# A new written order for a fused attention and squared-relu kernel, with the squares of its up-projection tiles moved between engines

## The chip, the cores and the metric

One core of one Trainium2 chip runs the whole program. The metric is the device time of one execution in microseconds (us), the median of several runs. Runs here differ by up to 1.4% for one kernel, so kernels are compared in runs that alternate on one chip. A ratio is the mean time of one kernel's fast runs over the mean of the other's fast runs of the same rounds, so it is not quite the ratio of the medians that stand beside it.

## The reference

```python
def _attn_ref(q, k, v):                       # q, k, v: 8 x 8 x 576 x 64
    scores = scale * np.matmul(q, k.transpose(0, 1, 3, 2))
    rel = pos[:, None] - pos[None, :]
    mask = (rel >= 0) & (rel < 64)            # a causal window of 64
    # ... softmax ...
    return np.matmul(attn, v)

def _moe_ref(x, w_in, w_out):                 # x: 4608 x 512, w_in: 512 x 2048
    h = np.maximum(x @ w_in, 0.0)
    return (h * h) @ w_out
```

Attention over a short window makes x; a two-layer network with a squared relu follows.

## The kernel before

Every piece of work is one word of a long text, and each engine executes its share of the words in the order of the text. A word's letters name the work, its numbers the tile, and what follows an @ the engine (D is DVE, A is ACT, P is POOL). Work is done in nine groups of 512 tokens. The words that matter:

- `S8`: scores of block 8 on PE; `E8.0` the exponentials on ACT; `M8.0` the mask on DVE; `V8.0` the values on PE; `N8.0` the norm on DVE.
- `U4.0` an up-projection chunk of 128 tokens (groups 0 and 1) with `R4.0`, its relu on ACT, and `Q4.0`, its square. `u2.0`, `r2.0`, `s2.0` are the same for groups 2 to 8, with 512 tokens.
- `O0.0.0`: the plain out-projection of group 0. From group 1 on it is done by seven products, `p1.1.0` and so on, whose inputs are in part sums of squares, `sa1.1.0@D`.

```python
SQUARE = "DAAP"                 # engine of the square of u tile f, by f % 4
SQUARE4 = ('DDDA', 'DADA')      # of the chunk, for group 0 and group 1

ps_up  = ctx.enter_context(tc.tile_pool(name="ps_up", bufs=2, space=bass.MemoryType.PSUM))
ps_out = ctx.enter_context(tc.tile_pool(name="ps_out", bufs=2, space=bass.MemoryType.PSUM))
ps_att = ctx.enter_context(tc.tile_pool(name="ps_att", bufs=4, space=bass.MemoryType.PSUM))

def square(key, a, b):
    # ... out: the tile of squares, hps: the up-projection in PSUM, hr: its relu in SBUF ...
    e = square_on(key, a, b)
    if e == "P":
        nc.gpsimd.tensor_tensor(out=out, in0=hr, in1=hr, op=ALU.mult)
        return
    if e == "A":
        nc.scalar.activation(out=out, in_=hr, func=AF.Square)
        return
    nc.vector.scalar_tensor_tensor(
        out=out, in0=hps[:], scalar=0.0, in1=hr, op0=ALU.max, op1=ALU.mult)
```

The square on DVE reads PSUM once more; the two others read the relu's copy. An up-projection has two PSUM buffers, so the tile after next waits until its buffer has been read for the last time.

The softmax here doesn't subtract the row's maximum and nothing guards it: scores larger than these inputs give would overflow.

Of the kernel before, what the change touches and what calls it, by code (L numbers as in the profile page):

```python
# [16 lines left out]
    lk0 lq0 dv0 ck0.0@A ck0.1@D ck0.2@P dv1 ck0.3@D W14 Tk0.0 Tk0.1 tk0.0@A li0 tk0.1@D cq0.0@A  # L17
    cq0.1@P cq0.2@D cq0.3@D Tq0.0 Tq0.1 tq0.0@A cv0@D dv2 tq0.1@D cn0@P cv1@A li1 S0 cs1@P S1
    E0.0 cn1@P E0.1 M0.0 E1.0 S2 M0.1 E1.1 M1.0 V0.0 ci0.0@P ci0.1@A dv3 V0.1 N0.0 N0.1 E2.0
    M1.1 cv2@P E2.1 li2 X0 M2.0 x0@D V1.0 cs2@P V1.1 M2.1 S3 N1.0 cn2@P U0.0@u N1.1 E3.0 E3.1 X1  # L20
    M3.0 V2.0 ci1.0@A ci1.1@P x1@D V2.1 li3 N2.0 U1.0@u R0.0 N2.1 M3.1 cv3@A X2 Q0.0 U0.1@o R1.0
    cs3@P x2@D U1.1@o Q1.0 R0.1 lo0 V3.0 Q0.1 R1.1 V3.1 U2.0@u N3.0 ci2.0@A ci2.1@P N3.1 U2.1@o
    Q1.1 R2.0 X3 Q2.0 lo1 R2.1 U0.2@u x3@D Q2.1 U1.2@u ci3.0@A ci3.1@P U3.1@o R0.2 R1.2 U0.3@o
    Q0.2 lk1 R3.1 Q1.2 U3.0@u R0.3 co0.0@D co0.1@P U2.2@u Q0.3 Q3.1 R3.0 U1.3@o R2.2 lq1 Q3.0
    Q2.2 U2.3@o R1.3 co1.0@P co1.1@D U3.2@u Q1.3 R2.3 U3.3@o R3.2 lo2 Q2.3 Q3.2 R3.3 O0.0.0
    ck1.0@D ck1.1@P ck1.2@A ck1.3@D Q3.3 O0.0.1 Tk1.0 lo3 Tk1.1 tk1.0@A O0.1.0 tk1.1@D cq1.0@P
    cq1.1@A O0.1.1 cq1.2@P cq1.3@A Tq1.0 dv4 Tq1.1 tq1.0@A tq1.1@D co2.0@P co2.1@A dv5 ta1.0@D
    S4 ta1.1@D S5 E4.0 dv6 O0.0.2 ta2.0@D E4.1 M4.0 E5.0 O0.1.2 M4.1 co3.0@P E5.1 dv7 co3.1@D S6
    M5.0 S7 M5.1 E6.0 cv4@P O0.0.3 ta2.1@D lk2 E6.1 M6.0 E7.0 cn4@P V4.0 M6.1 V4.1 E7.1 cv5@D
    O0.1.3 M7.0 Z0.0 cs5@P M7.1 N4.0 O0.2.0 Z0.1 cn5@P cv6@D lq2 N4.1 V5.0 cs6@P V5.1 ta3.0@D  # L30
    O0.3.0 cn6@P cv7@A N5.0 N5.1 V6.0 cs7@P V6.1 ta3.1@D O0.2.1 N6.0 z0.0 V7.0 N6.1 V7.1 O0.3.1
    N7.0 z0.1 N7.1 ck2.0@A ck2.1@P xx5 O0.2.2 ck2.2@D ck2.3@A ta4.0@D O0.3.2 ta4.1@D dv8 Tk2.0
    Tk2.1 tk2.0@A cq2.0@D cq2.1@P O0.2.3 cq2.2@D xx7 cq2.3@P tk2.1@D Tq2.0 Z0.2 Tq2.1 tq2.0@A
    O0.3.3 z0.2 tq2.1@D dv9 Z0.3 U4.0@u U4.1@u R4.0 z0.3 cv8@D S8 Q4.0 dv10 R4.1 cn8@P S9 E8.0
    U4.2@u E8.1 M8.0 dv11 E9.0 S10 M8.1 E9.1 M9.0 V8.0 E10.0 V8.1 M9.1 dk12 E10.1 N8.0 cv9@P
    Q4.1 M10.0 S11 M10.1 R4.2 U4.3@u N8.1 cs9@P dk13 E11.0 Q4.2 cn9@P E11.1 V9.0 V9.1 M11.0 R4.3
    cv10@P U5.0@u M11.1 dk14 N9.0 Q4.3 cs10@P N9.1 R5.0 U5.1@u cv11@D cn10@P xx9 Q5.0 cs11@P
    V10.0 R5.1 V10.1 N10.0 U5.2@u ek12@P Q5.1 N10.1 dk15 V11.0 R5.2 U5.3@u N11.0 ek13@P Q5.2
    V11.1 dq12 R5.3 p1.1.0 N11.1 Q5.3 ek14@P U6.0@u xx11 U6.1@u R6.0 p1.1.1 Q6.0 R6.1 dq13
    U6.2@u Q6.1 ek15@P va1.0 dq14 U6.3@u R6.2 p1.2.0 Q6.2 eq12@P R6.3 dq15 U7.0@u Q6.3 U7.1@u  # L40
    Kk3 R7.0 p1.2.1 Q7.0 R7.1 eq13@P sa1.3.0@D U7.2@u Q7.1 vc1.0 dv12 U7.3@u eq14@P R7.2
    sa1.3.1@D Q7.2 R7.3 vz1.0 eq15@P u2.0 sa1.1.0@D Q7.3 dv13 sa1.1.1@D u2.1 r2.0 sa1.2.0@D Kq3
    sa1.2.1@D r2.1 sa1.4.0@D s2.1 p1.6.0 sa1.4.1@D cv12@P p1.6.1 s2.0 dv14 cn12@P p1.7.0 va1.1
    dv15 u2.2 cv13@P u2.3 r2.2 cs13@P dk16 cn13@P p1.7.1 s2.2 r2.3 S12 dk17 va1.2 s2.3 S13 E12.0
    u2.8 E12.1 cv14@P M12.0 dk18 E13.0 u2.9 M12.1 E13.1 cs14@P M13.0 r2.8 V12.0 cv15@P M13.1
    dk19 V12.1 r2.9 S14 N12.0 cn14@P p1.5.0 N12.1 E14.0 s2.8 cs15@P E14.1 dq16 V13.0 ek16@P
    M14.0 V13.1 s2.9 u2.10 M14.1 N13.0 ek17@P dq17 N13.1 u2.11 r2.10 V14.0 s2.10 ek18@P V14.1
    N14.0 xx13 S15 r2.11 N14.1 u2.4 E15.0 s2.11 E15.1 p1.5.1 M15.0 r2.4 dq18 ek19@P M15.1 u2.5
    s2.4 eq16@P va1.3 dq19 V15.0 r2.5 u2.6 N15.0 s2.5 vc1.3 eq17@P V15.1 p1.4.0 r2.6 Kk4 N15.1
    s2.6 u2.7 u2.12 r2.7 vz1.3 p1.4.1 eq18@P r2.12 xx15 s2.7 p1.3.0 s2.12 vc1.2 eq19@P u2.13  # L50
    dv16 u2.14 r2.13 vz1.2 p1.3.1 s2.13 r2.14 Kq4 u2.15 sa2.1.0@D s2.14 sa2.3.0@D p2.1.0 r2.15
    sa2.2.0@D u3.0 s2.15 dv17 sa2.3.1@D sa2.4.0@D p2.1.1 r3.0 cv16@P sa2.1.1@D dv18 u3.1 va2.0
    s3.0 cn16@P sa2.2.1@D u3.2 r3.1 dv19 vc1.1 s3.1 sa2.4.1@D p2.2.0 r3.2 vz1.1 s3.2 S16 dk20
    S17 E16.0 cv17@P u3.3 E16.1 M16.0 cs17@P E17.0 dk21 p2.2.1 M16.1 E17.1 cv18@P M17.0 r3.3
    V16.0 M17.1 cn17@P V16.1 dk22 u3.8 N16.0 cs18@P N16.1 p2.6.0 vc2.0 cv19@P r3.8 dk23 cn18@P
    V17.0 s3.8 V17.1 cs19@P S18 N17.0 p2.6.1 ek20@P N17.1 vz2.0 E18.0 s3.3 E18.1 p2.7.0 M18.0
    xx17 va2.1 ek21@P S19 M18.1 u3.9 E19.0 dq20 ek22@P E19.1 u3.10 M19.0 r3.9 M19.1 V18.0 dq21
    s3.9 V18.1 ek23@P N18.0 p2.7.1 r3.10 N18.1 s3.10 u3.11 dq22 va2.2 u3.4 r3.11 dq23 p2.5.0
    s3.11 r3.4 p2.5.1 s3.4 eq20@P Kk5 u3.5 sa3.1.0@D eq21@P va2.3 u3.6 r3.5 sa3.2.0@D dv20 V19.0
    s3.5 vc2.3 V19.1 eq22@P p2.4.0 r3.6 N19.0 s3.6 N19.1 vz2.3 u3.7 eq23@P xx19 u3.12 r3.7  # L60
    p2.4.1 s3.7 r3.12 Kq5 p2.3.0 s3.12 vc2.2 u3.13 cv20@P u3.14 vz2.2 r3.13 cn20@P dv21 p2.3.1
    s3.13 r3.14 u3.15 sa3.3.0@D s3.14 dv22 sa3.3.1@D p3.1.0 r3.15 sa3.4.0@D u4.0 s3.15 dv23
    vc2.1 S20 r4.0 sa3.1.1@D u4.1 vz2.1 E20.0 s4.0 E20.1 p3.1.1 dk24 M20.0 r4.1 cv21@P M20.1 S21
    sa3.2.1@D s4.1 V20.0 cs21@P dk25 E21.0 V20.1 sa3.4.1@D u4.2 cv22@P E21.1 M21.0 va3.0 N20.0
    cn21@P p3.2.0 dk26 M21.1 r4.2 cs22@P N20.1 u4.3 s4.2 cv23@P dk27 p3.2.1 cn22@P r4.3 cs23@P
    u4.8 vc3.0 ek24@P dq24 p3.6.0 s4.3 r4.8 V21.0 s4.8 vz3.0 ek25@P V21.1 S22 N21.0 dq25 u4.9
    N21.1 E22.0 ek26@P E22.1 p3.6.1 M22.0 r4.9 xx21 M22.1 u4.10 ek27@P s4.9 va3.1 p3.7.0 r4.10
    dq26 eq24@P u4.11 s4.10 V22.0 dq27 r4.11 V22.1 N22.0 S23 N22.1 s4.11 p3.7.1 E23.0 Kk6 E23.1
    u4.4 M23.0 eq25@P va3.2 u4.5 M23.1 r4.4 p3.5.0 s4.4 dv24 r4.5 eq26@P u4.6 s4.5 dv25 p3.5.1
    eq27@P r4.6 V23.0 s4.6 sa4.1.0@D Kq6 V23.1 u4.7 N23.0 N23.1 p3.4.0 r4.7 sa4.2.0@D u4.12  # L70
    va3.3 s4.7 xx23 vc3.3 p3.4.1 cv24@P r4.12 u4.13 s4.12 vz3.3 cn24@P vc3.2 cv25@P dv26 p3.3.0
    r4.13 cs25@P u4.14 s4.13 cn25@P vz3.2 p3.3.1 r4.14 dv27 u4.15 s4.14 sa4.3.0@D sa4.3.1@D dk36
    u5.0 r4.15 sa4.4.0@D S24 s4.15 r5.0 vc3.1 p4.1.0 dk37 E24.0 s5.0 cv26@P E24.1 u5.1 M24.0
    M24.1 cs26@P vz3.1 p4.1.1 sa4.1.1@D r5.1 cn26@P dk38 sa4.2.1@D V24.0 s5.1 cv27@P V24.1 S25
    va4.0 N24.0 u5.2 sa4.4.1@D cs27@P dk39 E25.0 N24.1 ek36@P E25.1 p4.2.0 M25.0 r5.2 M25.1 dl28
    u5.3 s5.2 ek37@P p4.2.1 r5.3 dl29 u5.8 s5.3 vc4.0 dl30 p4.6.0 ek38@P r5.8 V25.0 s5.8 V25.1
    ek39@P S26 vz4.0 N25.0 u5.9 N25.1 E26.0 dl31 E26.1 eq28@P p4.6.1 M26.0 r5.9 M26.1 xx25 u5.10
    s5.9 va4.1 eq29@P p4.7.0 r5.10 Kk9 u5.11 s5.10 eq30@P V26.0 r5.11 V26.1 N26.0 S27 N26.1
    s5.11 p4.7.1 E27.0 dv36 E27.1 u5.4 M27.0 eq31@P va4.2 dv37 u5.5 M27.1 r5.4 p4.5.0 s5.4 r5.5
    Kq7 u5.6 s5.5 p4.5.1 r5.6 dv38 V27.0 s5.6 sa5.1.0@D V27.1 cv36@P u5.7 N27.0 N27.1 p4.4.0  # L80
    dv39 r5.7 sa5.2.0@D cv37@P u5.12 va4.3 s5.7 xx27 vc4.3 p4.4.1 r5.12 u5.13 s5.12 vz4.3 vc4.2
    p4.3.0 r5.13 dk40 cv38@P u5.14 s5.13 vz4.2 p4.3.1 r5.14 cv39@P dk41 u5.15 s5.14 sa5.3.0@D
    sa5.3.1@D S28 r5.15 dk42 u6.0 sa5.4.0@D E28.0 s5.15 vc4.1 E28.1 p5.1.0 r6.0 M28.0 vz4.1
    M28.1 u6.1 ek40@P sa5.1.1@D dk43 s6.0 p5.1.1 r6.1 sa5.2.1@D V28.0 s6.1 dv40 V28.1 sa5.4.1@D
    ek41@P S29 va5.0 u6.2 N28.0 E29.0 N28.1 dv41 E29.1 p5.2.0 M29.0 ek42@P r6.2 M29.1 u6.3 s6.2
    dv42 p5.2.1 r6.3 ek43@P dv43 u6.8 vc5.0 s6.3 p5.6.0 r6.8 cv40@P vz5.0 V29.0 s6.8 V29.1 Kk10
    u6.9 N29.0 cv41@P N29.1 p5.6.1 r6.9 cv42@P u6.10 s6.9 xx29 va5.1 p5.7.0 r6.10 cv43@P u6.11
    s6.10 dk32 p5.7.1 r6.11 dk33 u6.4 s6.11 va5.2 S30 r6.4 dk34 S31 E30.0 u6.5 s6.4 E30.1 M30.0
    E31.0 dk35 p5.5.0 M30.1 E31.1 M31.0 V30.0 r6.5 M31.1 V30.1 ek32@P dq32 u6.6 N30.0 s6.5 N30.1
# [25 lines left out]
def kernel(  # L115
# [10 lines left out]
    B, H, S, D = q.shape  # L126
    NT, DM = out.shape
    DFF = moe_w_in.shape[1]
    P = 128
# [27 lines left out]
    SQUARE = "DAAP"  # L157
    SQUARE4 = ('DDDA', 'DADA')
# [552 lines left out]
```

## Time and profile before

| | before |
|---|---|
| time, median of 3 runs | 308.19 us |
| PE, ACT, DVE, POOL busy | 94%, 60%, 69%, 45% of the span |
| PE's own work, at the spacing of its starts | 282.4 us |
| where PE's gaps lie | before 116 us |

PE executes 3198 matmuls and is the engine to watch. Its busy time contains each matmul's latency, so a small gap hides in it. I therefore use a second measure: the time lost in a stretch is its length less PE's work in it, priced as the prediction tells (its list of prices leaves out 112 transposes, the 6.2 us that its sum of 282.4 us has more). Over the program before, the profiled run lost 13.8 us up to U4.0 (of which some 7 us are the wait for the first load), 6.6 us from U4.0 to p2.1, 0.9 us from p2.1 to p8.1.

### The profile page before, as it was taken

The numbers are of one execution on the slowest core, as the hardware profiler recorded it, in microseconds if no ns is written. First come the engines' busy times: TensorE is split into PE (matmuls) and PEld (weight loads), VectorE is DVE, ScalarE is ACT, GpSimd is POOL, SyncE is SP. The second block draws the span as 40 slices with busy tenths as digits, with TensorE's granted clock in tenths as the row PEclk, the third lists the DMA queues.
The fourth block names the chain that finished last, engine by engine and source line by source line (L and its number), as shares of the span: only waits on it lengthen the run. The fifth ranks groups of instructions, "written<-read, shape, count | busy, mean of one in ns | idle before, by whom it ended". The sixth has DMA issues, their size and how long they took to land.

```text
span 308.1 us, 7884 instructions
## 1 busy us (share of the span) xinstructions
PE 289.9 (94%) x3198; PEld 200.3 (65%) x3198; DVE 211.7 (69%) x437; ACT 185.7 (60%) x319; POOL 139.2 (45%) x186
## 2 busy tenths in 40 slices
PE   8589987989979999999999999999999999999994
PEld 3469954578956465666666666666666656666683
DVE  3698679877296948974966696668496396633563
ACT  2667886386657656666766576566565665665500
POOL 3454354353246725943773595445353561111110
PEclk9659999998999999999999999999999999999999
DMA  7999999997989799999999999999999911310323
GB/s 240 305 359 367 355 273 289 177 233 143 173 205 206 136 179 236 212 183 239 248 191 204 227 207 201 211 234 217 219 181 232 219 38 36 104 34 2 68 70 102
DMA packets 159524, 59.76 MB, mean 194 GB/s; under 512 B 140544, under 2 KB 154880, under 8 KB 159488
## 3 DMA queue, kind: packets, MB, share of 16 engines
q1 hardware_dynamic: 159488, 59.26, 86.0%
q8 instruction: 25, 0.41, 0.6%
q14 instruction: 11, 0.09, 0.1%
HBM read 38.80 MB, written 9.44 MB: 157 GB/s over the span
## 4 chain that ended last, share of the span: by engine, by line
PE 75%; DVE 12%; DMA 5%; ACT 3%; POOL 1%; issue 1%; SPq 0%; DVEq 0%; ACTq 0%
PE pps L580 31%; PE hps L417 29%; PE hps L408 7%; DVE pm L354 4%; PE av L365 3%; DVE h_sum L540 3%; DMA kq_st<-in_q_dram 3%; DMA st<-in_v_dram 2%; PE sc L339 2%; DVE x_sb L376 2%; DVE h L450 1%; ACT pm L348 1%; PE ops L464 1%; ACT hrelu L429 1%; PE run_ps L297 1%
## 5 line engine op out<-in xcount | busy, mean ns | idle before, releaser
L429 ACT ACTIVATE hrelu<-hps 128x512 f32<-128x512 f32 x144 | 86.0, 598 | 78.8 <-PE hps L417 64.5
L417 PE MATMUL hps<-xT,w_in 128*128 128x512 f16 x448 | 111.9, 379 | 1.5 <-DVE h L450 1.5
L445 POOL TENSOR_TENSOR h<-hrelu 128x512 f16<-128x512 f32 x28 | 31.7, 1131 | 80.9 <-ACT hrelu L429 80.9
L417 PEld LDWEIGHTS <-w_in 128*128 128x128 f16 x448 | 42.1, 98 | 35.7 <-issue 1.9
L580 PEld LDWEIGHTS <-h_sum 128*128 128x128 f16 x512 | 49.3, 98 | 16.4 <-DVE h_sum L540 1.7
L580 PE MATMUL pps<-w_sum,h_sum 128*128 128x256 f16 x384 | 48.6, 273 | 0.9 <-DVE h_sum L540 0.9
L450 DVE SCALAR_TENSOR_TENSOR h<-hps,hrelu 128x512 f16<-128x512 f32 x48 | 32.8, 687 | 23.8 <-ACT hrelu L429 23.6
L580 PEld LDWEIGHTS <-h 128*128 128x128 f16 x384 | 37.0, 98 | 11.9 <-DVE osp L598 0.3
L448 ACT ACTIVATE h<-hrelu 128x512 f16<-128x512 f32 x68 | 43.0, 633 | 2.0
L348 ACT ACTIVATE pm<-sc 128x512 f16<-128x512 f32 x72 | 38.2, 605 | 8.0 <-PE sc L339 7.9
L540 DVE TENSOR_TENSOR h_sum<-h 128x1024 f16<-128x1024 f16 x32 | 23.9, 764 | 27.0 <-PE pps L580 26.1
L408 PE MATMUL hps<-xT,w_in 128*128 128x128 f16 x512 | 34.0, 230 | 0.3 <-ACT hrelu L429 0.3
L408 PEld LDWEIGHTS <-w_in 128*128 128x128 f16 x512 | 31.9, 103 | 1.1 <-issue 0.3
L580 PE MATMUL pps<-w_out,h 128*128 128x256 f16 x256 | 32.5, 273 | 0.0
L376 DVE TENSOR_TENSOR x_sb<-av,rden 128x256 f16<-128x256 f32 x72 | 30.6, 425 | 2.5
L354 DVE TENSOR_TENSOR pm<-pm,mask_inner 128x512 f16<-128x512 f16 x56 | 31.9, 599 | 0.1
L282 POOL CAST v_ev<-st 128x512 f16<-128x512 f32 x32 | 23.0, 723 | 15.8 <-DMA st<-in_v_dram 13.9
L598 DVE SCALAR_TENSOR_TENSOR osp<-pps,ws 128x512 f32<-128x512 f32 x32 | 21.9, 683 | 7.4 <-PE pps L580 7.4
L591 DVE SCALAR_TENSOR_TENSOR ws<-pps,ws 128x512 f32<-128x512 f32 x24 | 16.4, 684 | 12.6 <-PE pps L580 12.6
L286 POOL COPY v_od<-v_ev 64x512 f16<-64x512 f16 x24 | 18.0, 751 | 11.8 <-DVE v_ev L282 7.0
L365 PEld LDWEIGHTS <-pm 128*64 128x64 f16 x576 | 14.0, 115 | 13.3 <-issue 6.9
L271 POOL CAST k<-st 128x512 f16<-128x512 f32 x28 | 18.8, 690 | 7.1 <-DMA st<-in_k_dram 6.7
(63 smaller groups left out, 282.9 us busy)
## 6 DMA issues: line engine op xcount, KB each, us to landing
st<-in_v_dram SPq DMA_DIRECT2D x40, 256.0 KB, 4.3
st<-in_k_dram SPq DMA_DIRECT2D x28, 256.0 KB, 4.7
out_dram<-osp SPq DMA_DIRECT2D x28, 256.0 KB, 3.5
st<-in_q_dram SPq DMA_DIRECT2D x20, 256.0 KB, 4.6
w_st<-in_moe_w_in_dram SPq DMA_DIRECT2D x4, 1024.0 KB, 10.1
w_st<-in_moe_w_out_dram SPq DMA_DIRECT2D x4, 1024.0 KB, 9.0
kq_st<-in_k_dram SPq DMA_DIRECT2D x3, 1024.0 KB, 6.5
kq_st<-in_q_dram SPq DMA_DIRECT2D x3, 1024.0 KB, 7.6
```

Of the source, the lines that this page charges most:

```text
L348: nc.scalar.activation(out=pm[:], in_=live["s", i][hh][:], func=AF.Exp, scale=1.0 / float(D) ** 0.5)
L354: nc.vector.tensor_tensor(out=pms[i, hh][:], in0=pms[i, hh][:], in1=mask[:], op=ALU.min)
L365: nc.tensor.matmul(av[64 * blk:64 * blk + 64, h % 4, 0:65], pms[i, h % 2][:, h // 2, blk, :], vv[:, h, 0:65], start=True, stop=True)
L376: nc.vector.tensor_tensor(out=xs[i // 2][:, 2 * half:2 * half + 2, i % 2, :].rearrange("p c (b d) -> p c b d", d=D), in0=av[:, :, 0:D].rea ...
L408: nc.tensor.matmul(hps[:, f, :], w_in_q[fq][:, c, f * P:(f + 1) * P], xT_of(i // 4)[:, i % 4 // 2, c, a:a + P], start=(c == 0), stop=(c == ...
L417: nc.tensor.matmul(hps[:], w_in_q[f // 4][:, c, f % 4 * P:(f % 4 + 1) * P], xT_of(g)[:, :, c, :], start=(c == 0), stop=(c == DMC - 1))
L429: nc.scalar.activation(out=hrelu[:] if key == "U" else hrelu[:].rearrange("p (f t) -> p f t", t=P), in_=hps[:], func=AF.Relu, scale=H_SCAL ...
L445: nc.gpsimd.tensor_tensor(out=out, in0=hr, in1=hr, op=ALU.mult)
L448: nc.scalar.activation(out=out, in_=hr, func=AF.Square)
L450: nc.vector.scalar_tensor_tensor(out=out, in0=hps[:], scalar=0.0, in1=hr, op0=ALU.max, op1=ALU.mult)
L540: eng.tensor_tensor(out=out, in0=in0, in1=in1, op=op)
L580: nc.tensor.matmul(live["p", g, k][:, m, :], lhs, rhs, start=(f == 0), stop=(f == 7))
```

## The change

The intent was to lay the order out anew, with DVE taken as slower than the model had it, and to have fewer squares on DVE. Nearly every line of the text changed; matmuls and tiles stayed. Of the 1408 words 39 also changed their engine, all of them casts or copies. Cut to its core:

```diff
-SQUARE = "DAAP"
-SQUARE4 = ('DDDA', 'DADA')
+SQUARE = "AAAA"
+SQUARE4 = ('ADDA', 'AADA')
 ...
-    R5.3 p1.1.0 N11.1 Q5.3 ek14@P U6.0@u xx11 U6.1@u R6.0 p1.1.1 Q6.0 R6.1 dq13 U6.2@u Q6.1 ...
-    p1.2.1 Q7.0 R7.1 eq13@P sa1.3.0@D U7.2@u Q7.1 vc1.0 dv12 U7.3@u eq14@P R7.2 sa1.3.1@D ...
-    u2.0 sa1.1.0@D Q7.3 dv13 sa1.1.1@D u2.1 r2.0 sa1.2.0@D Kq3 sa1.2.1@D r2.1 sa1.4.0@D s2.1 p1.6.0
+    U6.1@u Q7.3 N11.0 eq12@P p1.1.0 R6.1 xx11 U6.0@u Q6.1 U6.2@u R6.0 dq15 p1.1.1 ...
+    p1.2.0 R7.2 U7.1@u Q7.2 dv12 u2.0 sa1.1.0@D R7.1 dv13 p1.2.1 Q7.1 sa1.2.0@D eq15@P r2.0
+    sa1.1.1@D u2.1 s2.0 Kq3 sa1.3.1@D u2.2 r2.1 sa1.2.1@D s2.1 sa1.4.0@D p1.6.0 ...
```

The PE words from the two texts (cut at p1.1.0):

```
old: U4.0 U4.1 S8 S9 U4.2 S10 V8.0 V8.1 S11 U4.3 V9.0 V9.1 U5.0 U5.1 V10.0 V10.1 U5.2 V11.0 U5.3 V11.1
new: U4.0 U4.3 U4.1 U4.2 S9 U5.2 S8 U5.1 V9.0 S10 U6.3 V8.0 V9.1 V8.1 U5.3 V10.0 V10.1 U5.0 S11 U7.0 U7.3 V11.1 V11.0 U6.1
```

## The prediction

> **What bounds the kernel now.** I read the totals and the 40 slices first, then PE's waits, then the busy times per stage, then the groups that the change touches.
>
> ```profile
> PE 289.9 (94%) x3198; PEld 200.3 (65%) x3198; DVE 211.7 (69%) x437; ACT 185.7 (60%) x319; POOL 139.2 (45%) x186
> PE   8589987989979999999999999999999999999994
> ACT  2667886386657656666766576566565665665500
> PEclk9659999998999999999999999999999999999999
> ```
>
> PE is the bound, and its gaps lie in the first twelve slices (some 90 us) and in the last one. Who PE waits for, after 90 us and before:
>
> ```profile
> PE av L365 <- DVE x_sb L376: 1.3, 4, 0.5
> PE pps L580 <- DVE h_sum L540: 0.9, 1, 0.9
> PE hps L417 <- DVE h L450: 0.7, 1, 0.7
> PE sc L339 <- DVE x_sb L376: 0.2, 1, 0.2
> ...
> PE run_ps L297 <- ACT q L265: 1.9, 1, 1.9
> PE av L365 <- POOL v_od L286: 1.5, 3, 0.6
> PE warm L457 <- DVE gate L652: 1.3, 1, 1.3
> ```
>
> After 90 us PE waits 3.1 us in 218, always for DVE. I cut the span at PE's first instruction of each stage: first four-chunk up-projection (U0.0), first plain out-projection (O0), second group's up-projection (U4.0), first product (p1.1), second group of products (p2.1), last group (p8.1). The windows view (stretch, length, then busy us of PE, weight loads, DVE, ACT, POOL, granted clock, DMA):
>
> ```profile
> 0.00:19.20 19.20, 13.41 (x146) 7.78 (x146) 11.39 (x36) 9.24 (x14) 9.12 (x20) 0.77 0.99 285
> 19.20:37.30 18.10, 18.10 (x304) 17.67 (x301) 13.76 (x32) 14.15 (x24) 6.21 (x7) 0.87 1.05 364
> 37.30:61.60 24.30, 21.28 (x260) 12.29 (x258) 21.12 (x45) 15.35 (x25) 11.70 (x14) 1.00 1.00 253
> 61.60:76.00 14.40, 12.97 (x257) 11.57 (x255) 11.51 (x29) 10.53 (x20) 6.93 (x11) 0.88 0.86 189
> 76.00:116.10 40.10, 37.72 (x439) 26.45 (x434) 26.77 (x52) 26.21 (x46) 19.45 (x26) 1.00 0.99 180
> 116.10:291.50 175.40, 173.87 (x1697) 113.71 (x1696) 118.49 (x236) 109.03 (x190) 84.59 (x108) 1.00 0.84 173
> 291.50:308.10 16.60, 12.59 (x113) 10.78 (x111) 8.62 (x14) 1.19 (x2) 1.20 (x1) 0.98 0.27 80
> ```
>
> From 116 us to 291 us PE has no gap worth a change: nothing gained on another engine can show there. All there is to win lies in the first 116 us.
>
> **What can be won.** Busy time flatters PE, since a matmul's latency counts, so I price PE's work by the spacing of starts in the timeline: 0.864 us for a four-matmul up tile or out-projection step, 0.875 us for half a product, 0.9 us for a 16-matmul chunk, 0.41 us for scores of a block, 0.25 us for half its values, 6 us for the warm-up. Over the program that is 282.4 us, before and after alike: the change has the same 3198 matmuls. The other 308.1 - 282.4 = 25.7 us are the tail after the last matmul (4.0), and 21.7 us of start, waits and half clock. Of these some 7 us pass until k has come and is cast, and no order saves them. So the most that a new order could give is about 14 us; a realistic one gives a third of it.
>
> **What the Trainium skill says.**
> - "ScalarE: Activation LUTs", What ACT_TABLE_LOAD costs: an ACTIVATE with immediate scale and bias takes 186 ns + 0.833 ns per element, 613 ns at 512. The trace has 633 ns (square) and 598 ns (relu): it agrees. Relu, square and exp share one table set here, for the trace has a single table load: no reload is added.
> - "GPSIMD Engine Reference", Engine selection: elementwise work with two inputs is about twice as slow on GPSIMD as on VectorE. Here 1131 ns against 687 ns, 1.65 times.
> - "SBUF — State Buffer", Who interferes with whom: a DVE instruction with two SBUF inputs contends with a GpSimd one that reads SBUF. The trace agrees: masks take 414 ns where no POOL instruction overlaps and 652 ns where one does; the 1024-wide sums 687 and 840 ns.
>
> **The change, part by part.** The code puts all 112 squares of the plain up tiles (groups 2 to 8) on ACT; the short description speaks of POOL too, but no square is left there. The groups concerned:
>
> ```profile
> L429 ACT ACTIVATE hrelu<-hps 128x512 f32<-128x512 f32 x144 | 86.0, 598 | 78.8 <-PE hps L417 64.5
> L445 POOL TENSOR_TENSOR h<-hrelu 128x512 f16<-128x512 f32 x28 | 31.7, 1131 | 80.9 <-ACT hrelu L429 80.9
> L450 DVE SCALAR_TENSOR_TENSOR h<-hps,hrelu 128x512 f16<-128x512 f32 x48 | 32.8, 687 | 23.8 <-ACT hrelu L429 23.6
> L448 ACT ACTIVATE h<-hrelu 128x512 f16<-128x512 f32 x68 | 43.0, 633 | 2.0
> L354 DVE TENSOR_TENSOR pm<-pm,mask_inner 128x512 f16<-128x512 f16 x56 | 31.9, 599 | 0.1
> ```
>
> Of the 112, 28 leave DVE and 28 leave POOL. Of the 32 four-chunk squares 20 were on DVE and are 12. So POOL loses 28 x 1.131 = 31.7 us and falls to about 107; DVE loses 36 x 0.687 = 24.7 us and falls to about 187, or less, as its masks and sums meet fewer POOL reads (if 40 of them go from 0.65-0.84 to 0.41-0.69 us, some 8 us more). ACT gains 64 x 0.633 = 40.5 us and goes to about 226 us, 73% of the span, most loaded after PE. A square on ACT also frees its PSUM buffer at the end of the relu, 0.69 us earlier than one on DVE, which reads PSUM again.
>
> The order decides where this falls. I walked through both written orders and summed each engine's work between the same landmarks (PE / ACT / DVE in us, durations from the trace; before, then after):
> - start to U0.0: 10.7 / 8.6 / 11.1, then 10.9 / 11.0 / 10.9. A chain of load, cast, transpose, scores, exp, values, norm. One more v tile (256 KB) is loaded ahead of the first weights, and three blocks of scores come before U0.0. Before 19.2 us; I take 20.0.
> - U0.0 to O0: 16.1 / 16.4 / 15.0, then 16.7 / 18.8 / 13.0. Before 18.1 us. ACT is now the longest: 19.0.
> - O0 to U4.0: 21.1 / 16.7 / 25.1, then 19.7 / 15.7 / 21.2. Before 24.3 us, set by DVE. Now DVE and PE nearly level: 21.5.
> - U4.0 to p1.1: 10.8 / 11.5 / 12.5, then 14.9 / 18.1 / 12.2. Before 14.4 us. Four more chunks come ahead of p1.1, and ACT sets the pace: 18.0.
> - p1.1 to p2.1: 36.9 / 27.4 / 27.4, then 32.5 / 28.2 / 21.1. Before 40.1 us, 3.2 lost, largely to DVE. Less DVE and less POOL: 34.0, so 1.5 lost.
> - p2.1 to p8.1: PE 174.6, then 175.5; ACT 115.7, then 146.0 (83% of PE's). Before 175.4 us, 0.8 lost. DVE's load falls, ACT's queue is fuller: 176.5.
> - p8.1 to the end: the same chain of products and sums, 16.6.
>
> Sum: 20.0 + 19.0 + 21.5 + 18.0 + 34.0 + 176.5 + 16.6 = **305.6 us**, 2.6 us (0.8%) below 308.19. (The profiled span, 308.1, and the median agree, so I take the sum as a time.) Most of ACT's 40 us and all of POOL's 32 us therefore lie beside PE and cost or give nothing; the gain is the DVE work taken from two early stages, partly paid back where ACT takes over.
>
> **The rivals.**
> 1. *ACT becomes the bound.* ACT works in order, and a relu behind a square and two exps holds a PSUM buffer of which there are two. From U4.0 to p2.1 ACT has 46.3 us of work for PE's 47.4. For it: 97% there, and 89% from p3.1 to p4.1 (26.4 for 29.7). Against: before, PE lost 0.3 us at most to ACT relus, with ACT two thirds as loaded as PE in the middle; and I compared, for each up tile, PE's work between a buffer's two uses with ACT's and DVE's work in its way: from p2.1 on 2 of the tiles fall short, by 1.2 us in all (before: none). If it comes, each group loses 1 us more: 310 to 313 us.
> 2. *The order is simply better.* It was laid out with DVE reckoned slower than modelled, which is what the contention above asks for. The head's waits (21.7 us less 7) could fall by half: 300 to 302 us. Against: the three sets of such covers that I summed (up buffers, product buffers, scores to values) fall short by 19.4 us before and 16.3 after, which is only 3 us better, and chains of the first 20 us stay.
> 3. *Nothing shows.* PE has no gap in 175 us of 308, and the head is set by loads and by the half clock (0.5 granted from 10.4 to 24.1 us): 307 to 309 us.
>
> **Range and chances.** Rivals 1 and 3 pull up, 2 down, each stage estimate is good to about 1 us and the head to 2: 301.5 to 311 us, 8 in 10. Faster by 2% means under 302.0, which needs rival 2 nearly whole: 0.14. Slower means over 314.4, which needs rival 1 in every group: 0.05. Within 2%: 0.81.
>
> **What would show it right or wrong.** Right: ACT 224 to 228 us busy, 132 squares at about 633 ns, no POOL square, DVE below 187 with masks under 560 ns in the mean; U4.0 about 60.5 us, p2.1 about 112.5, and the last two stages unchanged. Wrong: PE waits for ACT relus or exps of more than 3 us after 116 us (rival 1); p2.1 before 109 us (rival 2); masks still near 600 ns, which would say that the casts and not the squares were what DVE met; or a second stretch of half clock in the head, 1.7 us each.

## The result

The changed kernel took 304.69 us in the median of 4 runs (303.55 to 305.72), the kernel before 308.29 us in 4 (307.87 to 308.62). The ratio is 0.9883, with a 95% interval of 0.9845 to 0.9921: 1.2% faster, within the 2%.

The page of the changed kernel: totals, then the busy tenths of 40 slices.

```profile
PE 287.6 (95%) x3198; PEld 196.4 (65%) x3198; DVE 187.1 (62%) x395; ACT 220.7 (73%) x386; POOL 107.8 (36%) x161
...
PE   7489997999999999999999999999999999999994
...
ACT  2879975699799679578886785688865887877710
...
PEclk9759999999999999999999999999999999999999
```

PE has gaps in the first seven slices alone (some 50 us) and in the last. ACT is at 5 to 9 tenths through the middle, POOL and DVE are freer. Whom PE waits for, after 60 us and then before it:

```profile
PE pps L580 <- DVE osp L598: 0.4, 1, 0.4
PE av L365 <- DVE rden L375: 0.3, 1, 0.3
PE av L365 <- DVE x_sb L376: 0.2, 1, 0.2
...
PE run_ps L297 <- ACT q L265: 2.1, 1, 2.1
PE ops L464 <- POOL w_out L278: 1.7, 1, 1.7
```

No wait for an ACT relu is left in the list. The same seven stages as in the prediction, in the windows view (stretch, length, busy us of PE, weight loads, DVE, ACT, POOL, granted clock, DMA share, GB/s):

```profile
0.00:19.30 19.30, 12.30 (x150) 7.58 (x151) 11.45 (x38) 11.62 (x19) 8.21 (x19) 0.79 0.98 283
19.30:37.30 18.00, 17.75 (x314) 17.47 (x313) 11.57 (x25) 15.98 (x28) 6.57 (x8) 0.94 1.04 365
37.30:59.30 22.00, 20.06 (x236) 10.50 (x234) 17.70 (x39) 14.55 (x24) 12.47 (x15) 1.00 1.02 275
59.30:74.90 15.60, 15.29 (x331) 13.95 (x329) 11.56 (x28) 15.04 (x28) 9.76 (x15) 1.00 1.25 199
74.90:107.80 32.90, 32.54 (x368) 22.56 (x366) 20.86 (x42) 26.87 (x49) 13.27 (x21) 1.00 1.08 206
107.80:285.40 177.60, 177.24 (x1702) 113.45 (x1701) 106.22 (x214) 134.27 (x238) 57.48 (x84) 1.00 0.85 172
285.40:301.80 16.40, 12.43 (x113) 10.86 (x111) 7.74 (x12) 2.34 (x4) 0.00 (x0) 0.99 0.27 81
```

From U4.0 to p2.1 (the fourth and fifth rows) the changed kernel takes 48.5 us, the kernel before took 54.5. PE's work there is nearly the same, 47.4 and 47.7 us. ACT is busy 15.0 of 15.6 us in the fourth row, and yet PE hardly waits. The groups that the change touches:

```profile
L429 ACT ACTIVATE hrelu<-hps 128x512 f32<-128x512 f32 x144 | 85.3, 595 | 47.5 <-PE hps L417 43.4
...
L448 ACT ACTIVATE h<-hrelu 128x512 f16<-128x512 f32 x132 | 82.7, 634 | 3.3
...
L354 DVE TENSOR_TENSOR pm<-pm,mask_inner 128x512 f16<-128x512 f16 x56 | 29.4, 550 | 7.0 <-ACT pm L348 6.7
```

The 132 squares on ACT take 634 ns each, as foretold. The POOL squares are gone.

This table holds the argument of the rest: the time lost in the one profiled run, by stretch (length less PE's priced work), with the ratio to the kernel before from all the timed runs. Of the 6.6 us of the kernel before, up to 1.7 are a second stretch of half clock (3.4 us long), of which more below.

| kernel | lost to U4.0 | U4.0 to p2.1 | p2.1 to p8.1 | median us | ratio to before (95%) |
|---|---|---|---|---|---|
| before | 13.8 | 6.6 | 0.9 | 308.3 | 1 |
| changed | 11.9 | 1.1 | 2.2 | 304.7 | 0.988 (0.985 to 0.992) |
| changed, control | 12.9 | 0.9 | 2.6 | 305.2 | 0.988 (0.985 to 0.991) |
| new order, old squares | 13.5 | 3.5 | 5.6 | 310.7 | 1.007 (1.003 to 1.010) |
| old order, new squares | 13.2 | 5.8 | 0.6 | 308.1 | 0.997 (0.995 to 1.000) |
| new to p2.1, then old | 13.1 | 1.3 | 1.2 | 303.7 | 0.985 (0.983 to 0.988) |
| old to p2.1, then new | 12.9 | 4.4 | 2.8 | 309.1 | 1.003 (1.001 to 1.006) |
| old to U4.0, then new | 13.0 | 1.4 | 2.7 | 305.6 | 0.992 (0.989 to 0.995) |
| new to U4.0, then old | 12.5 | 5.4 | 1.1 | 309.6 | 1.004 (1.000 to 1.009) |
| new from U4.0 to p2.1 alone | 14.5 | 1.7 | 1.1 | 304.5 | 0.987 (0.984 to 0.989) |

The five rows that mix the two orders all have the new squares.

### The profile page after: what moved, and what is told of

It reads as the page before. It is cut to its first block, busy times and chain, and to the rows that moved or that the text cites. A ratio compares the mean times of both kernels' runs of the same rounds, so it can differ in the third digit from the quotient of the medians.

```text
span 301.8 us, 7861 instructions
## 1 busy us (share of the span) xinstructions
PE 287.6 (95%) x3198; PEld 196.4 (65%) x3198; DVE 187.1 (62%) x395; ACT 220.7 (73%) x386; POOL 107.8 (36%) x161
## 4 chain that ended last, share of the span: by engine, by line
PE 80%; DVE 6%; DMA 6%; ACT 3%; SPq 2%; issue 1%; POOL 1%; ACTq 0%
PE pps L580 32%; PE hps L417 31%; PE hps L408 6%; PE av L365 5%; DMA w_st<-in_moe_w_out_dram 3%; PE ops L464 3%; PE sc L339 2%; DMA st<-in_v_dram 2%; DVE pm L354 2%; ACT hrelu L429 2%; SPq L183 1%; DVE h_sum L540 1%; DVE h L450 1%; ACT h L448 1%; POOL w_out L278 1%
## 5 line engine op out<-in xcount | busy, mean ns | idle before, releaser
L417 PE MATMUL hps<-xT,w_in 128*128 128x512 f16 x448 | 110.5, 380 | 0.0
L448 ACT ACTIVATE h<-hrelu 128x512 f16<-128x512 f32 x132 | 82.7, 634 | 3.3
L417 PEld LDWEIGHTS <-w_in 128*128 128x128 f16 x448 | 41.8, 98 | 35.7
L282 POOL CAST v_ev<-st 128x512 f16<-128x512 f32 x36 | 25.5, 708 | 69.2 <-DMA st<-in_v_dram 56.8
L354 DVE TENSOR_TENSOR pm<-pm,mask_inner 128x512 f16<-128x512 f16 x56 | 29.4, 550 | 7.0 <-ACT pm L348 6.7
L408 PE MATMUL hps<-xT,w_in 128*128 128x128 f16 x512 | 32.5, 223 | 0.3 <-DVE xT L393 0.2
L580 PE MATMUL pps<-w_out,h 128*128 128x256 f16 x256 | 31.7, 273 | 0.4 <-DVE osp L598 0.4
L376 DVE TENSOR_TENSOR x_sb<-av,rden 128x256 f16<-128x256 f32 x72 | 30.5, 424 | 2.5
L408 PEld LDWEIGHTS <-w_in 128*128 128x128 f16 x512 | 30.4, 100 | 0.9 <-issue 0.2
L365 PEld LDWEIGHTS <-pm 128*64 128x64 f16 x576 | 14.0, 112 | 16.7 <-issue 8.5
L271 POOL CAST k<-st 128x512 f16<-128x512 f32 x28 | 18.1, 659 | 15.7 <-DMA st<-in_k_dram 14.9
L271 POOL CAST q<-st 128x512 f16<-128x512 f32 x24 | 14.8, 616 | 21.3 <-DMA st<-in_q_dram 21.1
L375 DVE RECIPROCAL rden<-av 128x4 f32<-128x4 f32 x72 | 12.6, 175 | 13.6 <-PE av L365 13.5
L365 PE MATMUL av<-v_ev,pm 128*64 128x65 f16 x384 | 20.1, 202 | 0.5 <-DVE pm L354 0.4
```

The source lines that it names most:

```text
L271: copier(e)(out=kq16(key, i // 4)[:, :, i % 4, :].rearrange("p a (b d) -> p a b d", d=D), in_=st[key, i][:].rearrange("p (a b) d -> p a b ...
L282: copier(e)(out=v_evs[slot(i)][:, :, 0:D], in_=st["v", i][:])
L354: nc.vector.tensor_tensor(out=pms[i, hh][:], in0=pms[i, hh][:], in1=mask[:], op=ALU.min)
L365: nc.tensor.matmul(av[64 * blk:64 * blk + 64, h % 4, 0:65], pms[i, h % 2][:, h // 2, blk, :], vv[:, h, 0:65], start=True, stop=True)
L376: nc.vector.tensor_tensor(out=xs[i // 2][:, 2 * half:2 * half + 2, i % 2, :].rearrange("p c (b d) -> p c b d", d=D), in0=av[:, :, 0:D].rea ...
L408: nc.tensor.matmul(hps[:, f, :], w_in_q[fq][:, c, f * P:(f + 1) * P], xT_of(i // 4)[:, i % 4 // 2, c, a:a + P], start=(c == 0), stop=(c == ...
```

## The experiments

Theory A said that the squares taken from DVE make the gain; theory B, that the new order does; theory C, that fewer POOL reads do, since DVE and POOL get in each other's way. First the changed kernel again, as a control on the same chip.

> The changed kernel once more, as the control that the next three are compared with on one chip. Every theory: a ratio to the kernel before of 0.985 to 0.992, ACT 220 us busy, DVE 187 us, POOL 108 us. What may differ is where the half clock falls in the first 25 us; if the stretch of half clock near 68 us of the kernel before comes and goes between runs, it is chance and not the change.

It ran 305.18 us against 309.12 us, a ratio of 0.9878, so the result repeats. The eleven runs of the kernel before in the rounds of the control had granted clocks of 0.970 to 0.994. The two lowest, 0.970 and 0.971, took 310.2 and 310.1 us, the others 307.3 to 309.4. Of its 22 runs beside the later experiments two more were so low (0.972 and 0.971; 309.3 and 310.1 us). The profiled run of before, with its second stretch of half clock from 68.4 to 71.8 us, is one of the low kind (0.971, 309.83 us). The second stretch seems to come by chance in a few runs; a mean clock doesn't tell where the half clock lay, so this is inferred. It is part of the profile of before, but not of its median, and so not what the change removed.

**The order without the squares, and the squares without the order.**

```diff
 # in the changed kernel
-SQUARE = "AAAA"
-SQUARE4 = ('ADDA', 'AADA')
+SQUARE = "DAAP"
+SQUARE4 = ('DDDA', 'DADA')
```

> The new written order with the squares on the engines of before (20 of the four-chunk ones and 28 of the plain ones on DVE, 28 on POOL). Theory A, the squares taken from DVE make the gain: about 308 us, ratio 0.997 to 1.005, DVE back at some 211 us busy. Theory B, the order itself makes it: 304 to 305.5 us, ratio 0.985 to 0.991. Theory C, fewer POOL reads make it: like A, with the masks and sums of DVE slower than in the changed kernel. My guess is 306.5, a half each.

```diff
 # in the kernel before
-SQUARE = "DAAP"
-SQUARE4 = ('DDDA', 'DADA')
+SQUARE = "AAAA"
+SQUARE4 = ('ADDA', 'AADA')
```

> The old written order with the squares of the changed kernel (all plain ones on ACT, 12 of the four-chunk ones on DVE). Theory A: 304.5 to 306 us, ratio 0.986 to 0.993, the gain without the new order. Theory B: 308 us or more, since ACT then has 46 us of squares and relus more at places that were laid out for less of it; PE waits for ACT relus would appear after 116 us. My guess is 307.

The new order with the old squares is slower than the kernel before: 310.74 us, ratio 1.0067. The old order with the new squares gains next to nothing: 308.11 us, 0.9974. My guesses of 306.5 and 307 were both too low. (The squares took ACT 40 us more in the second, 83.1 for 43.0, not the 46 of my expectation.) Neither A nor B is right alone: each half is worth nothing or less, and the two together 1.2%.

PE's waits after 60 us in the new order with the old squares:

```profile
PE hps L417 <- DVE h L450: 1.4, 3, 0.6
PE pps L580 <- DVE osp L598: 1.2, 1, 1.2
PE hps L408 <- DVE h L450: 0.9, 1, 0.9
PE av L365 <- DVE pm L354: 0.5, 1, 0.5
```

PE waits for squares on DVE, which hold the up-projection's PSUM buffer longer than the new order allows. For comparison, the stretch from 60 us to p2.1, first before, then in the old order with new squares:

```profile
PE pps L580 <- DVE h_sum L540: 0.9, 1, 0.9
PE sc L339 <- DVE x_sb L376: 0.9, 2, 0.8
PE hps L417 <- DVE h L450: 0.8, 1, 0.8
PE av L365 <- DVE x_sb L376: 0.5, 2, 0.3
```

```profile
PE pps L580 <- DVE h_sum L540: 1.1, 2, 0.7
PE av L365 <- DVE x_sb L376: 0.8, 3, 0.3
PE sc L339 <- DVE x_sb L376: 0.7, 1, 0.7
PE hps L417 <- DVE h L450: 0.5, 1, 0.5
```

DVE has less work in this stretch (33.2 us busy instead of 38.3), yet PE waits for the same four things for about as long. These waits are for chains: relu, square and sum before a product; exp, mask, values and norm before the next scores take the buffers. In the old order with the new squares DVE stood idle for 2.5 us before the masks that start at 64.4 us and for 2.6 us before the sums that start at 83.2 us. It then ran through with hardly a gap to 67.2 and 89.4 us, where PE's waits for x_sb and h_sum end. So the squares that were taken away had not been in the way of these two, and a lighter DVE doesn't shorten them. Other work for PE in between can cover them.

**POOL's share.**

```diff
 # in the changed kernel
-SQUARE = "AAAA"
+SQUARE = "AAAP"
```

> The changed kernel with one plain square in four back on POOL (28 of them), DVE as changed. Theory C, POOL reads slow DVE: at least half of the gain lost, 306 us or more, masks and 1024-wide sums longer by 5 per cent or more. Theories A and B: within 0.3 per cent of the changed kernel, since PE does not wait for POOL and ACT has room again; if ACT were near its bound in the changed kernel, it would even be faster by 1 us.

It ran 306.16 us, 0.9916 to the kernel before, against the control's 0.9878 in the same rounds: some 1.2 us slower, a third of the gain, with intervals that just overlap. The group of masks, first with POOL's squares back, then in the old order with the new squares:

```profile
L354 DVE TENSOR_TENSOR pm<-pm,mask_inner 128x512 f16<-128x512 f16 x56 | 37.7, 703 | 4.7 <-ACT pm L348 4.5
```

```profile
L354 DVE TENSOR_TENSOR pm<-pm,mask_inner 128x512 f16<-128x512 f16 x56 | 27.6, 513 | 3.8 <-ACT pm L348 3.6
```

28 squares on POOL lengthen the masks from 550 ns (567 in the control) to 703 ns, and DVE is busy 195.3 us instead of 187.1. So theory C's mechanism is there, but it costs only some 0.4%: a part of the whole and not the gain.

**Where in the order the gain lies.** Each of these kernels takes one text up to a word and then what is left of the other text, in its order. All have the new squares. Theory D: the new order pays between U4.0 and p2.1, and costs a little after it. Theory E: it pays because it was laid out as one.

```diff
 # the changed kernel's text up to p2.1.0, then the old text's remaining words
 ... u2.14 s2.13 vz1.2 p1.3.1 Kq4 r2.14
-p2.1.0 s2.14 sa2.1.0@D u2.12 sa2.3.0@D dv16 sa2.2.0@D ...
+u2.12 r2.12 s2.12 dv16 sa2.1.0@D s2.14 sa2.3.0@D p2.1.0 ...
```

> Squares as changed; the new order up to the second group of products (p2.1), and from there what is left in the old order. Theory D, the order pays between U4.0 and p2.1 only (PE lost 5.8 us there with the old order and new squares, 0.9 us in the control) and costs some 2 us after p2.1 (0.6 us lost with the old order, 2.6 with the new): 303 us, ratio 0.981, faster than the changed kernel by some 2 us. Theory E, the new order pays everywhere because it was laid out as one: 305 us or more, the cut itself costing.

```diff
 # the old text up to p2.1.0, then the new text's remaining words
 ... r2.14 Kq4 u2.15 sa2.1.0@D s2.14 sa2.3.0@D
-p2.1.0 r2.15 sa2.2.0@D u3.0 s2.15 ...
+r2.15 s2.15 p2.1.0 sa2.2.0@D p2.1.1 sa2.3.1@D u3.0 ...
```

> The reverse: the old order up to p2.1, the new one after it, squares as changed. Theory D: slower than both parents, about 310 us, ratio 1.003, 5 us lost between U4.0 and p2.1 and 2 to 2.6 us after p2.1. Theory E: between the parents, 306 to 307 us.

```diff
 # the old text up to U4.0, then the new text's remaining words
 ... O0.3.3 z0.2 tq2.1@D dv9 Z0.3
-U4.0@u U4.1@u R4.0 z0.3 cv8@D S8 ...
+U4.0@u z0.3 U4.3@u R4.0 Q4.0 cv8@P R4.3 U4.1@u ...
```

> The old order up to the second group's up-projection (U4.0, some 61 us), the new one after it, squares as changed. Theory D: as the changed kernel, 305 to 306 us, ratio 0.988 to 0.991, since the new order of the first 60 us gains next to nothing (13.2 us lost before U4.0 with the old order, 12.9 with the new). If the order of the first 60 us is what pays: 308 us.

```diff
 # the new text up to U4.0, then the old text's remaining words
 ... Tq2.0 Z0.3 Tq2.1 tq2.0@D
-U4.0@u tq2.1@A z0.3 U4.3@u xx7 R4.0 Tk2.1 ...
+Tk2.1 xx7 tk2.1@D tq2.1@D U4.0@u U4.1@u R4.0 z0.3 ...
```

> The new order up to U4.0 and the old one after it, squares as changed. Theory D: as the old order with new squares, 307.5 to 308.5 us, ratio 0.995 to 0.999, and 5 to 6 us lost between U4.0 and p2.1. If the order of the first 60 us is what pays: 305 us.

Measured: 303.69, 309.13, 305.57 and 309.61 us. Theory D foretold 303, about 310, 305 to 306, and 307.5 to 308.5; the last is 1 us too low. Four of that kernel's six runs had low clocks (0.971 to 0.978) and took 309.5 to 311.7 us; the two at 0.981 and 0.982 took 307.9 and 307.4, as foretold. As the table shows, the time lost between U4.0 and p2.1 is 0.9 to 1.7 us wherever the new order stands there, and 4.4 to 5.8 us wherever the old one does with the same squares. What lies before U4.0 makes no such difference. After p2.1 the new order loses 2.2 to 2.8 us and the old one 0.6 to 1.2.

The first of the four was meant to beat both kernels. Its runs lie between 303.0 and 303.9 us, the lowest median, though its ratio (0.9854) overlaps with the changed kernel's (0.9878 and 0.9883), and they weren't timed in the same rounds. I call it the best measured, not shown to be better.

**That stretch alone, and the squares piece by piece.**

```diff
 # the old text; from U4.0 to p2.1.0 the new text's words; then the old text's remaining words
 ... O0.3.3 z0.2 tq2.1@D dv9 Z0.3
+U4.0@u z0.3 U4.3@u R4.0 Q4.0 cv8@P ...   # new text
 ...
+u2.12 r2.12 s2.12 dv16 sa2.1.0@D s2.14 sa2.3.0@D p2.1.0 ...   # old text again
```

> Squares as changed; the old order everywhere but from U4.0 to p2.1, where the new one stands: one part of the reordering alone. Theory D (that stretch is what pays): 303.5 to 304.5 us, ratio 0.985, with at most 1.5 us lost in the stretch where the old order loses 5.8. If the rest of the new order is needed too: 306 us or more.

It ran 304.45 us, ratio 0.9868: the new order of this one stretch, with the new squares, brings the whole gain. (The stretch also has `cv8` and `cv11` on POOL instead of DVE, two casts of about 0.4 us; that part wasn't tried alone.) PE's waits there are down to this (line numbers of this kernel are three lower: its L405, L362, L372 and L373 are L408, L365, L375 and L376 of the changed kernel):

```profile
PE hps L405 <- DVE h L447: 0.3, 1, 0.3
PE av L362 <- DVE x_sb L373: 0.3, 1, 0.3
PE av L362 <- DVE rden L372: 0.3, 1, 0.3
```

The wait for h_sum and the wait of the scores for x_sb are gone. DVE is busy 31.7 us in it, close to the 33.2 of the old order with the same squares.

```diff
 # in the changed kernel
-SQUARE = "AAAA"
+SQUARE = "DAAA"
```

> The changed kernel with one plain square in four back on DVE (28 of them), POOL and the four-chunk squares as changed. The new order with all old squares is 1.9 per cent (5.6 us) slower than the changed kernel, and POOL's 28 alone cost 0.4 per cent (1.0 us). If DVE's load in the later groups is what the new order can't bear, this one takes most of the other 4.6 us: 308 us or more, with PE waiting for DVE squares after 110 us. If the four-chunk squares do: within 1 us of the changed kernel.

```diff
 # in the changed kernel
-SQUARE4 = ('ADDA', 'AADA')
+SQUARE4 = ('DDDA', 'DADA')
```

> The changed kernel with the four-chunk squares (groups 0 and 1) on the engines of before, so 8 more of them on DVE in the first 110 us and none else. If the head's DVE load is what counts: 307 us or more, all of it lost before p2.1. If the later groups': within 1 us of the changed kernel. My guess is 306.5, with 1.5 us lost before p2.1, as ACT gets 5 us less there and was close to its bound.

With 28 plain squares back on DVE the time is 305.76 us (0.9924); with 8 chunk squares back it is 308.00 us (0.9986). I had guessed 306.5 for the second, and had named both outcomes for the first. On the face of it eight squares of the first two groups, 5.5 us of DVE work, cost more than 28 of the later ones, 19.2 us of it. Measured from the control's 0.988 the three parts cost 0.4% (POOL), 0.4% (plain on DVE) and 1.1% (chunks), which adds up to the 1.9% by which the new order with all the old squares is slower than the control. (These two ran in another call than the control, so each is good to about 0.4%.) The wait that the chunks bring, after 58 us:

```profile
PE hps L408 <- DVE h L450: 1.2, 1, 1.2
```

In its profiled run 1.1 us of the delay was already there at U0.0 (20.6 us against the control's 19.5), ahead of any square, and the first half clock lasted 13.7 us instead of 10.2. Its stretches therefore overstate the chunks' part. The timed runs may do so too: all six had clocks of 0.975 to 0.978, against 0.981 to 0.989 for five of the control's six. Set against the two runs of the kernel before with low clocks in the same rounds (0.971 and 0.977; 310.09 and 309.49 us), the ratio would be about 0.995 and not 0.9986. A low mean clock doesn't always cost time, though: the runs of "new to p2.1, then old" at 0.974 to 0.977 were no slower than those at 0.982 and 0.983. So the chunk squares cost something, PE's wait of 1.2 us for one of them shows it, but how much of the 1.1% is theirs stays open, and with it whether they cost more than the later ones.

**A trial that failed.**

```diff
 # the old text up to O0.0.0; then the new text's remaining words up to p2.1.0; then the old ones
 ... U3.3@o R3.2 lo2 Q2.3 Q3.2 R3.3
-O0.0.0 ck1.0@D ck1.1@P ck1.2@A ck1.3@D Q3.3 O0.0.1 ...
+ck1.0@P ck1.1@A ck1.2@D ck1.3@P Tk1.0 Tk1.1 tk1.0@D tk1.1@A O0.0.0 ...
```

> Squares as changed; old order up to O0 (there 35.7 us in two runs, against 37.3 to 38.3 with the new), new order from O0 to p2.1, old order after it. If stages add up as theory D has it: 302 us, ratio 0.979, better than any so far by 1.5 us. If the first 36 us are set by loads, so that what comes early waits later: 303.5 to 304.5 us, as the new order up to p2.1 with the old one after it.

It took 307.48 us, 3 us more than the worse of my two cases. The stages did not add up. PE's waits from 36 to 62 us (line numbers again three lower than in the changed kernel):

```profile
PE av L362 <- DVE pm L351: 3.2, 3, 2.0
PE run_ps L294 <- ACT k L262: 1.1, 1, 1.1
```

Part of the loss is the cut's own: it puts the transposes of the second group's k ahead of O0.0.0, where PE waits 1.1 us for the cast of k. O0.0.0 starts at 38.5 us, against 35.7 to 35.9 in the three other profiles with the old order up to there and a first half clock of the same 10.2 us. Later PE stood still for 2.0 us for masks that DVE was doing at about 0.77 us each instead of 0.41, and the clock was then halved from 53.6 to 57.0 us. The control's masks are as slow there (four in 3.07 us), and it has a wait of 1.4 us for them; the changed kernel's first profile has one of 1.7 us for a weight cast on POOL, in nearly the same place. One might think that the loads set the pace there and that each order only chooses which wait shows it. But the DMA share is 1.03 up to 36 us and only 0.86 from 36 to 62 us in the failed trial, against 0.99 to 1.04 in the control and the changed kernel, which speaks against it for this run. The wait for k, the waits for masks and the half clock after them are what its trace shows. The half clock alone can't be the reason: of the six timed runs five had clocks of 0.969 to 0.978, but the sixth, at 0.983, took the longest, 308.35 us. Why the masks came so late for PE stays open.

## Why the prediction was right or wrong

The time was foretold as 305.6 us and came out at 304.69, in the range and on the right side. The cause that it gave was wrong, and errors that went opposite ways helped the number. By its steps:

| stage | predicted us | changed | control |
|---|---|---|---|
| start to U0.0 | 20.0 | 19.3 | 19.5 |
| U0.0 to O0 | 19.0 | 18.0 | 18.4 |
| O0 to U4.0 | 21.5 | 22.0 | 22.3 |
| U4.0 to p1.1 | 18.0 | 15.6 | 15.8 |
| p1.1 to p2.1 | 34.0 | 32.9 | 32.5 |
| p2.1 to p8.1 | 176.5 | 177.6 | 178.1 |
| p8.1 to the end | 16.6 | 16.4 | 16.4 |
| sum: the span | 305.6 | 301.8 | 303.0 |

- **PE as the bound, and no gain after 116 us: right.** The stretch from p2.1 on even became 2 us longer, 0.9 us of it work that the new order has there, the rest lost.
- **"Four more chunks come ahead of p1.1, and ACT sets the pace: 18.0": the mis-sized term.** It took 15.6 us. ACT's words of this stage do have 18.4 us of durations in the trace (18.1 foretold), and only one of them, the square `Q7.3`, was still to start when p1.1 began. But successive activations overlap in the records: 17.6 us of durations within the stage make 15.0 us of busy time. So ACT did run nearly full, and the sum of durations, without the overlap, overstated it by some 2.6 us.
- **The base.** I took the span of 308.1 us for the median of 308.19. A run's time is about 1.7 us above its span (303.55 for 301.8, 309.83 for 308.1), so the profile of before was of a run slower than the median, with its second stretch of half clock. This and the last point went opposite ways: the stages summed to 3.8 us too many against the first profile's span, while the time was 0.9 us off. That it came so close is in part luck.
- **"The gain is the DVE work taken from two early stages": wrong as a cause.** I put the 3.2 us lost from p1.1 to p2.1 "largely to DVE", because DVE is what the waits name. With DVE's work taken away and the old order kept, 5.8 us were still lost from U4.0 to p2.1. With the new order in that stretch alone, 1.7 us were. What the waits named was the last link of a chain, and the order of that stretch is what saved the time. That it did so by putting PE work beside the chain fits the texts (3.5 us of it instead of 1.7 between the last chunk of group 1 and p1.6.0, the first product that needs the sums of squares) and the waits that went away, but no run moved that work alone. The squares were needed as well, since the new order has no room for a DVE square that holds a PSUM buffer (3.5 us lost there with the old squares).
- **Engine sums: right but for ACT.** POOL 107.8 us (foretold about 107), DVE 187.1 (about 187 or less), ACT 220.7 (224 to 228). ACT's groups grew by the 40 us that I reckoned: the squares went from 43.0 to 82.7. Its busy time grew by 35.0, since successive activations overlap in the records: the durations of all ACT instructions sum to 198.9 us before and 241.3 after, and 116 and 192 pairs of them overlap, by 13.1 and 20.6 us in all. That is 7.5 us over 76 more pairs, 98 ns each. The Trainium skill gives about 93 ns ("ScalarE: Activation LUTs", What ACT_TABLE_LOAD costs): I had cited the page's duration and not its overlap.
- **"Masks under 560 ns": half right.** The inner masks came to 550 ns, from 599, but the sixteen first masks went to 708 from 585, so all 72 take 585 ns in the mean, from 596. The test that I set for POOL's part gave no answer. The experiment did: with 28 squares on POOL too the inner masks take 703 ns. The new order by itself lengthens them, from 513 ns in the old order with the same squares; 23 times a mask meets one of POOL's casts of v there, 15 times in the old order.
- **The rivals.** ACT as the bound (1) did not come: no wait for a relu above 0.3 us after 60 us. "The order is simply better" (2) was nearer the truth than my main line, for the wrong reason: it did not halve the head's waits but took away those from U4.0 to p2.1, and only together with the squares. "p2.1 before 109 us", the sign that I set for it, came true (107.8). Nothing shows (3) did not come.

## What to carry to other kernels

A wait names the last link of a chain; before taking work off the engine that is named, see whether that engine was busy when the chain began, because if not, less work on it won't shorten the chain; other work laid beside it may hide it. An order and an assignment of work to engines should be tried together: here each alone was worth at most 0.3%, and together 1.2%. When an engine's durations are summed to bound a stage, their overlap must come off: here 17.6 us of activations took 15.0 us.

## What the Trainium skill lacked or had wrong

- "SBUF — State Buffer", Who interferes with whom, says that the later of two colliding instructions waits, but gives no size for this pairing. Here a mask on DVE took 414 to 418 ns where no POOL instruction overlapped and 636 ns in the mean where one did (777 ns in the run with all the old squares in the new order). POOL suffers too: one weight cast in the stretch where DVE was adding weights took 1.87 us, against 1.04 to 1.13 us.
- "TensorE: Matmul & The Clock Gate", What's actually happening, ties the half clock to an idle window of about 3.4 us (the page tells further down of short idles that bring it too, without a size). In these traces 3.4 us of half clock followed PE gaps of 1.0 and 2.2 us in the failed trial, from 50.1 to 53.5 us, and gaps of 0.3, 0.3, 0.3 and 0.9 us in the profile of before, counted from the spacing of starts. But it did not follow a gap of 1.9 us in the changed kernel or gaps of 0.4, 0.3, 0.3 and 0.9 us in the old order with the new squares, so the gaps' size alone doesn't decide.
- No page says how long the half clock of the first 25 us may last. In the 14 profiles here it lasted 6.8, 10.2 or 13.7 us, which is worth knowing beside effects of 1 us.
- No page compares a kernel's device time with the span from its first to its last instruction; here the time was longer by about 1.7 us (1.65 to 1.99).
